# A mixer kernel: channel weights, GpSimd sums and one weight split queued behind named instructions

## The chip, the cores and the metric

The kernel runs on one core of one Trainium2 chip. The metric is device time in microseconds (us), taken as the median of several executions; a profiled execution of the same program gives the span from its first to its last instruction and the trace that is read here.

## The reference, cut to what matters

Eight batches, eight heads, 576 tokens, 64 channels a head. A linear attention (softmax of q over the channels, softmax of k over the tokens) makes x; two small networks follow, one over tokens and one over channels.

```python
q_s = exp(q - max(q, -1)); q_s = q_s / (sum(q_s, -1) + 1e-9)
k_s = exp(k - max(k, 2));  k_s = k_s / (sum(k_s, 2) + 1e-9)
x = q_s @ (k_s^T v)                       # (8, 576, 512) over all heads
h = relu(x^T @ w_tok1) @ w_tok2           # w_tok1 576x256, w_tok2 256x576
u = x + h^T
out = u + relu(u @ w_ch1) @ w_ch2         # w_ch1 512x1536, w_ch2 1536x512
```

The weights arrive as 8-byte numbers, so each piece of them (128x512) has to be narrowed on the chip.

## The kernel before, in words

**Units.** The attention is cut into 32 units, one for a batch and a pair of heads. A unit passes through `softmax_k` and `softmax_q` (VectorE and ScalarE), the transposes and the k-v product (`stage_qT`, `stage_kv`), `stage_y`, `stage_h1`, and two halves of `stage_u`. Each half ends by emptying its PSUM bank into u: a ScalarE copy makes the high part uh (L365), a VectorE subtraction the low part ul (L366). The first eight units are "early": they run in a loop of their own, before any step of the channel network is issued, with buffers of their own (`early_pools`).

**Steps.** The tokens are cut into nine groups of 512. For a group g and a block f of 128 hidden channels, `ch1(g, f)` does 12 matmuls into a bank and drains it into h2h (ScalarE, L379) and h2l (VectorE, L380); `ch2` does 12 more matmuls, one step later. The steps run in the order (0, 0..3), (1, 0..11), (0, 4..11), then groups 2 to 8. At the end of the first four steps the sums of group zero are copied to `part` (L409); the rest of group zero is added at its end. Units 8 to 31 are spread over the steps by a table (`todo`).

**Weights.** `load_ch(f)` loads the pieces of w_ch1 and w_ch2 for block f. For each piece there is a DMA into `stg` issued by SyncE (L154), then `narrow` (VectorE L162, ScalarE L163, VectorE L164, L165, L167, L169), then `split` into a high and a low part (ScalarE L102, VectorE L103). Blocks 0 and 1 are loaded in the early loop, after units 5 and 6; blocks 2 to 11 are loaded at the steps 0 to 9, one at each. Step 4 + f is the first that needs a block f of 4 or more. `split_tok1` splits w_tok1, which the early units use whole, for the later units; it stands after unit 4 in the loop.

**Sums on GpSimd.** `residual` makes u = uh + ul ready for the output. For group one and later it is one GpSimd addition for each quarter into a `stg` buffer (L402). For group zero it is two for each quarter, into `part` (L395, L396).

**Order.** The program's text gives priorities. A scheduler with its own timeline orders each engine's queue: it lets an instruction go ahead of earlier text when its engine would be free and its data ready in that timeline. On the chip each engine then keeps to its queue's order.

Of the kernel before, what the change touches and what calls it, by code (L numbers as in the profile page):

```python
# [1 line left out]

# [6 lines left out]
F32 = mybir.dt.float32  # L9
F32R = mybir.dt.float32r  # L10
U32 = mybir.dt.uint32
AF = mybir.ActivationFunctionType
ALU = mybir.AluOpType
AX = mybir.AxisListType

P = 128
# [4 lines left out]
def attn_mixer_kernel(ctx: ExitStack, tc: tile.TileContext, q, k, kt, v, wt, out, dims):  # L21
# [3 lines left out]
    nc = tc.nc  # L25
    B, H, S, D, TOK, DM, DCH, wide = dims
    NJ = DM // P
    NF = DCH // P
# [7 lines left out]
    NE = 2 * NJ  # L36
    F_HEAD, F_MORE = 4, 8

    const = ctx.enter_context(tc.tile_pool(name="const", bufs=1))
    sm = ctx.enter_context(tc.tile_pool(name="sm", bufs=2))  # L40
    stg = ctx.enter_context(tc.tile_pool(name="stg", bufs=2))
    cv = ctx.enter_context(tc.tile_pool(name="cv", bufs=2))
# [42 lines left out]
    def c2_rows(f0, f1):  # L85
        late = ctx.enter_context(tc.tile_pool(name=f"late{f0}", bufs=1))
        h_ = late.tile([P, f1 - f0, DM], F32R, name=f"c2h{f0}")
        l_ = late.tile([P, f1 - f0, DM], F32R, name=f"c2l{f0}")
        for f in range(f0, f1):
            c2[f] = h_[:, f - f0, :], l_[:, f - f0, :]  # L90
# [6 lines left out]
    def f32(ap):  # L97
        return ap.bitcast(F32)

    def split(hi, lo, src, lo_eng):  # L100

        nc.scalar.copy(hi, src)  # L102
        lo_eng.tensor_tensor(lo, src, f32(hi), op=ALU.subtract)  # L103
# [3 lines left out]
    def ps_unit(dtype=F32):  # L107

        pools = unit_banks[0]
        pool, name = pools[turn[0] % len(pools)]  # L110
        turn[0] += 1
        return pool.tile([P, 512], dtype, name=name)
# [33 lines left out]
    def load_weights(i, n=CW, out=None):  # L146

        if not wide:
            t = out if out is not None else cv.tile([P, C1 * P], F32, name="cv_s")[:, 0:n]
            nc.sync.dma_start(t, wt[i][:, 0:n])  # L150
            return t
        conv.append(conv.pop(0))
        raw = conv[-1][0].tile([P, CW, 2], U32, name="stg")
        nc.sync.dma_start(raw[:, 0:n, :].rearrange("p n w -> p (n w)"), wt[i][:, 0:n].bitcast(U32))  # L154
        return narrow(raw, n, out)
# [30 lines left out]
    def split_tok1():  # L186
        split(w1h, w1l, w1f[:, 0:C, :], nc.vector)
        split(w1th, w1tl, w1t, nc.vector)

    def load_tok2():  # L190
        for n in range(NT):
            split(w2h[:, n, 0:S0], w2l[:, n, 0:S0], load_weights(AT_T2 + n), nc.vector)
        t = load_weights(AT_TAIL + 1, NT * TL).rearrange("p (n t) -> p n t", n=NT)
        split(w2h[:, :, S0:S], w2l[:, :, S0:S], t, nc.vector)

    def load_ch(f):
        h_, l_ = (w[:, f].rearrange("p n m -> p (n m)") for w in (c1h, c1l))
        split(h_, l_, load_weights(AT_C1 + f), nc.vector)
        split(*c2[f], load_weights(AT_C2 + f), nc.vector)
# [137 lines left out]
    uT = [slots[i] for i in (0, 1, 2, 1, 0, 2, 1, 0, 2)]  # L337
    assert len(uT) == NG

    def stage_u(u, half):  # L340
        b, j = u["b"], u["j"]
        edge = (b + 1) * CW - b * S
        cut = min(max(edge, S - 320), 320)
        n0, n1 = ((0, cut), (cut, S))[half]
        N = n1 - n0
        ns = slice(n0, n1)
        t = ps_unit()
        if u["early"]:
            mm = [(u["kvf"], u["qt"][:, ns])]
        else:  # L350
            mm = [(u["kvh"], u["qth"][:, ns]), (u["kvh"], u["qtl"][:, ns]), (u["kvl"], u["qth"][:, ns])]
        for n in range(NT):
            mm += [
                (u["hh"][:, n, :], w2h[:, n, ns]),
                (u["hh"][:, n, :], w2l[:, n, ns]),
                (u["hl"][:, n, :], w2h[:, n, ns]),
            ]
        for i, (a, w) in enumerate(mm):
            nc.tensor.matmul(t[:, 0:N], a, w, start=(i == 0), stop=(i == len(mm) - 1))  # L359
        for g, a0, a1 in ((b, n0, min(n1, edge)), (b + 1, max(n0, edge), n1)):  # L360
            if a0 < a1:
                at = b * S + a0 - g * CW
                uh, ul = (x[:, j, at : at + a1 - a0] for x in uT[g])
                src = t[:, a0 - n0 : a1 - n0]
                nc.scalar.copy(uh, src)  # L365
                nc.vector.tensor_tensor(ul, src, f32(uh), op=ALU.subtract)  # L366


    def ch1(g, f):
        hh = hpool.tile([P, CW], F32R, name="h2h")  # L370
        hl = hpool.tile([P, CW], F32R, name="h2l")
        t = ps_h.tile([P, 512], F32, name="ps_h")
        i = 0
        for n in range(NJ):
            uh, ul = (x[:, n, :] for x in uT[g])
            for a, w in ((c1h, uh), (c1l, uh), (c1h, ul)):
                nc.tensor.matmul(t, a[:, f, n, :], w, start=(i == 0), stop=(i == 3 * NJ - 1))  # L377
                i += 1
        nc.scalar.activation(hh, t, AF.Relu)  # L379
        nc.vector.scalar_tensor_tensor(hl, t, 0.0, f32(hh), op0=ALU.max, op1=ALU.subtract)  # L380
        return hh, hl

    def ch2(acc, f, first, last, hh, hl):

        for n, o in enumerate(acc):
            cs = slice(n * P, (n + 1) * P)
            for i, (a, w) in enumerate(((c2[f][0], hh), (c2[f][1], hh), (c2[f][0], hl))):
                nc.tensor.matmul(o, a[:, cs], w, start=(first and i == 0), stop=(last and i == 2))  # L388

    def residual(g, n):  # L390

        uh, ul = (x[:, n, :] for x in uT[g])
        if g == 0:
            t = part[:, n, :]
            nc.gpsimd.tensor_tensor(t, t, f32(uh), op=ALU.add)  # L395
            nc.gpsimd.tensor_tensor(t, t, f32(ul), op=ALU.add)  # L396
            res[n] = t
            return
        if n % 2 == 0:
            t = stg.tile([P, CW, 2], U32, name="stg").rearrange("p n w -> p (n w)").bitcast(F32)  # L400
            res[n], res[n + 1] = t[:, 0:CW], t[:, CW : 2 * CW]
        nc.gpsimd.tensor_tensor(res[n], f32(uh), f32(ul), op=ALU.add)  # L402

    res = {}

    def out_end(g, acc, whole):
        for n, o in enumerate(acc):
            if not whole:
                nc.scalar.copy(part[:, n, :], o)  # L409
                continue  # L410
            nc.vector.tensor_tensor(res[n], o, res[n], op=ALU.add)
            nc.scalar.dma_start(out[g, n], res[n])
# [4 lines left out]
    def begin(n):  # L417
        if n < NU and n not in units:
            units[n] = load_unit(n // NJ, n % NJ)

    def soft(n):
        if n < NU:
            softmax_k(units[n])
            softmax_q(units[n])

    def pe_stages(n):
        def s1():
            stage_qT(units[n])
            stage_kv(units[n])

        def s2():
            stage_y(units[n])

        def s3():
            stage_h1(units[n])
            stage_u(units[n], 0)

        def s4():
            stage_u(units[n], 1)

        return s1, s2, s3, s4
# [19 lines left out]
    for n in range(NE):  # L461
        st = pe_stages(n)
        st[0]()
        st[1]()
        if n == 0:
            load_tok2()
        if n + 2 < NE:
            begin(n + 2)
            soft(n + 2)
        st[2]()  # L470
        st[3]()
        if n == NE - 4:
            split_tok1()
        if NE - 3 <= n < NE - 1:
            load_ch(n - (NE - 3))
    early_pools.close()
    del v_ring[1:], kv_ring[1:]
    ld = ctx.enter_context(tc.tile_pool(name="ld", bufs=2))
# [35 lines left out]
            put(x, fn)  # L514

    pend = None
    to_load = 2
    for i, (g, f) in enumerate(steps):
        if to_load < NF and (i < F_HEAD or g == 1):
            if to_load == F_MORE:  # L520
                more_pools.close()
                conv[:] = [(stg, cv)]
                c2_rows(F_MORE, NF)
            load_ch(to_load)
            to_load += 1
        h = ch1(g, f)
        for fn in todo.pop(i, []):
            fn()
        if pend is not None:
            ch2(*pend[1:])  # L530
            if pend[0] != g:
                out_end(*pend[:2], i != F_HEAD)
        for fn in todo.pop(i + 0.5, []):
            fn()
        last = i + 1 == len(steps) or steps[i + 1][0] != g
        if pend is None or pend[0] != g:
            acc = [ps_o.tile([P, CW], F32, name="ps_o") for _ in range(NJ)]
        pend = (g, acc, f, pend is None or pend[0] != g, last, *h)
        if last and i != F_HEAD - 1:
            for n in range(NJ):  # L540
                residual(g, n)
# [60 lines left out]
```

## Time and profile before

| what | value |
|---|---|
| median of 3 runs | 851.43 us (850.38 to 853.24) |
| profiled execution, its own time | 851.01 us |
| span of its instructions | 849.2 us |
| mean granted TensorE clock | 0.995 |
| busy: TensorE, VectorE, ScalarE, GpSimd | 807.7, 495.6, 323.8, 132.5 us |
| chain that ended last: TensorE, VectorE, DMA | 76%, 14%, 5% |

The engines are called PE (TensorE matmuls), PEld (its weight loads), DVE (VectorE), ACT (ScalarE), POOL (GpSimd) and SP (SyncE). A row of the timeline gives the start, the time taken, engine, line, operation, output<-input and the count of merged instructions; in brackets stand the idle time of the engine before it and what ended it. A DVE instruction's time is some 0.07 us longer than the distance to the next one's start when it runs undisturbed, since neighbours overlap.

### The profile page before, as it was taken

What the parts mean: (1) busy time and instruction counts of PE and PEld (TensorE: products, weight loads), DVE (VectorE), ACT (ScalarE), POOL (GpSimd) and SP (SyncE); (2) the same over time, 40 slices, a digit from 0 to 9 for tenths busy, and PEclk for the clock granted to TensorE, in tenths of its full rate; (3) what the DMA queues carried; (4) which work ended last, traced back from release to release, by engine and by line L of the source; (5) the groups of instructions that cost most, each with busy time, mean ns of one, the idle gap of its engine ahead of it and who ended that gap; (6) DMA issues with size and microseconds to landing.
All of it is one profiled execution on the core that took longest, in us unless ns stands there. A gap on an engine that the chain in (4) does not pass through costs nothing.

```text
span 849.2 us, 11727 instructions
## 1 busy us (share of the span) xinstructions
PE 807.7 (95%) x4464; PEld 671.8 (79%) x4464; DVE 495.6 (58%) x1076; ACT 323.8 (38%) x749; POOL 132.5 (16%) x104
## 2 busy tenths in 40 slices
PE   3779997998999999999999999999999999999997
PEld 2567885877888888888888888888888888888885
DVE  7899899988665555565557555755566322112111
ACT  4576552444553444344434344444344321011110
POOL 0000015042221111131113011311131102001000
PEclk9999999999999999999999999999999999999999
DMA  8543742223223222322213122312131001001001
GB/s 264 171 137 93 237 136 81 93 76 110 62 77 95 61 61 61 110 61 61 61 40 97 51 60 61 98 58 61 46 95 46 15 1 50 1 0 50 1 1 50
DMA packets 60632, 63.54 MB, mean 75 GB/s; under 512 B 40864, under 2 KB 40992, under 8 KB 60576
## 3 DMA queue, kind: packets, MB, share of 16 engines
q1 hardware_dynamic: 55392, 53.36, 21.5%
q10 hardware_dynamic: 5184, 9.44, 3.0%
q8 instruction: 35, 0.57, 0.3%
q14 instruction: 21, 0.17, 0.1%
HBM read 53.35 MB, written 9.44 MB: 74 GB/s over the span
## 4 chain that ended last, share of the span: by engine, by line
PE 76%; DVE 14%; DMA 5%; issue 2%; ACT 1%; POOL 1%; DVEq 0%; SPq 0%; POOLq 0%
PE ps_h L377 29%; PE ps_o L388 29%; PE ps_h L359 7%; PE ps_h L316 5%; PE ps_h L256 2%; DMA stg<-in_w 2%; DMA q_t<-in_q 2%; DVE q_t L302 2%; DVE stg L167 2%; DVE cv_s L169 1%; PE ps_h L324 1%; DVE cv_s L164 1%; DMA out<-stg 1%; PE ps_h L222 1%; DVE stg L165 1%
## 5 line engine op out<-in xcount | busy, mean ns | idle before, releaser
L380 DVE SCALAR_TENSOR_TENSOR h2l<-ps_h,h2h 128x512 fp32r<-128x512 f32 x108 | 74.0, 686 | 177.0 <-ACT h2h L379 177.0
L388 PE MATMUL ps_o<-h2h,c2h 128*128 128x512 f32 x432 | 169.9, 396 | 4.4 <-ACT h2h L379 4.4
L377 PE MATMUL ps_h<-uh,c1h 128*128 128x512 f32 x432 | 171.3, 396 | 0.0
L377 PE MATMUL ps_h<-ul,c1h 128*128 128x512 f32 x432 | 170.9, 396 | 0.0
L377 PE MATMUL ps_h<-uh,c1l 128*128 128x512 f32 x432 | 170.4, 394 | 0.0
L388 PE MATMUL ps_o<-h2h,c2l 128*128 128x512 f32 x432 | 169.8, 393 | 0.0
L379 ACT ACTIVATE h2h<-ps_h 128x512 fp32r<-128x512 f32 x108 | 64.3, 596 | 248.3 <-PE ps_h L377 240.7
L388 PE MATMUL ps_o<-h2l,c2h 128*128 128x512 f32 x432 | 154.6, 396 | 2.3 <-DVE h2l L380 2.3
L302 DVE COPY q_t<-cv_s 32x160 f32<-32x160 f32 (+1 forms) x264 | 72.8, 276 | 63.5 <-POOL ql L103 60.2
L388 PEld LDWEIGHTS ps_o<-h2h,c2h 128*128 128x128 f32 x432 | 81.7, 189 | 22.2 <-ACT h2h L379 5.3
L377 PEld LDWEIGHTS ps_h<-ul,c1h 128*128 128x128 f32 x432 | 81.3, 188 | 19.3
L388 PEld LDWEIGHTS ps_o<-h2l,c2h 128*128 128x128 f32 x432 | 79.6, 188 | 19.9 <-DVE h2l L380 3.6
L388 PEld LDWEIGHTS ps_o<-h2h,c2l 128*128 128x128 f32 x432 | 81.7, 189 | 16.8
L377 PEld LDWEIGHTS ps_h<-uh,c1h 128*128 128x128 f32 x432 | 81.3, 188 | 17.1
L377 PEld LDWEIGHTS ps_h<-uh,c1l 128*128 128x128 f32 x432 | 81.5, 189 | 16.8
L225 POOL TENSOR_TENSOR k_t<-k_t,mb 128x640 f32<-128x640 f32 x24 | 37.8, 1574 | 280.4 <-ACT mb L224 280.3
L402 POOL TENSOR_TENSOR stg<-uh,ul 128x512 f32<-128x512 f32 x32 | 41.6, 1324 | 155.8 <-DMA out<-stg 76.8
L103 POOL TENSOR_TENSOR ql<-q_t,qh 128x640 fp32r<-128x640 f32 x24 | 37.9, 1580 | 96.6 <-ACT qh L102 59.7
L233 DVE TENSOR_REDUCE st<-q_t 128x10 f32<-128x640 f32 x32 | 26.2, 818 | 42.5 <-DMA q_t<-in_q 42.5
L235 ACT ACTIVATE q_t<-q_t 128x640 f32<-128x640 f32 x32 | 23.6, 739 | 49.0 <-DVE q_t L234 49.0
L302 ACT COPY q_t<-cv_s 32x128 f32<-32x128 f32 (+1 forms) x120 | 36.8, 307 | 1.5
L359 PE MATMUL ps_h<-w2h,hh 128*128 128x256 f32 (+1 forms) x112 | 33.1, 303 | 1.4 <-ACT hh L331 1.4
(140 smaller groups left out, 1162.1 us busy)
## 6 DMA issues: line engine op xcount, KB each, us to landing
stg<-in_w SPq DMA_DIRECT2D x28, 512.0 KB, 3.7
kt_t<-in_kt SPq DMA_DIRECT2D x32, 320.0 KB, 3.5
q_t<-in_q SPq DMA_DIRECT2D x32, 320.0 KB, 3.0
v_t<-in_v SPq DMA_DIRECT2D x64, 128.0 KB, 3.0
out<-stg ACTq DMA_DIRECT2D x32, 256.0 KB, 2.7
k_t<-in_k SPq DMA_DIRECT2D x24, 320.0 KB, 3.6
v_t<-in_v SPq DMA_DIRECT2D x32, 32.0 KB, 3.1
out<-part ACTq DMA_DIRECT2D x4, 256.0 KB, 4.6
```

Source lines behind the costliest of these rows:

```text
L103: lo_eng.tensor_tensor(lo, src, f32(hi), op=ALU.subtract)
L225: nc.gpsimd.tensor_tensor(kx, kx, mb.unsqueeze(1).broadcast_to([P, C1, P]), op=ALU.subtract)
L233: nc.vector.tensor_reduce(st[:, 0, :], qt, axis=AX.X, op=ALU.max)
L235: nc.scalar.activation(qc, qc, AF.Exp)
L302: eng(qx[ys, 0:n, xs], turned[xs, 0:n, ys])
L316: nc.tensor.matmul(y[:, 0:TOK], a, w, start=(i == 0), stop=(i == len(mm) - 1))
L359: nc.tensor.matmul(t[:, 0:N], a, w, start=(i == 0), stop=(i == len(mm) - 1))
L377: nc.tensor.matmul(t, a[:, f, n, :], w, start=(i == 0), stop=(i == 3 * NJ - 1))
L379: nc.scalar.activation(hh, t, AF.Relu)
L380: nc.vector.scalar_tensor_tensor(hl, t, 0.0, f32(hh), op0=ALU.max, op1=ALU.subtract)
L388: nc.tensor.matmul(o, a[:, cs], w, start=(first and i == 0), stop=(last and i == 2))
L402: nc.gpsimd.tensor_tensor(res[n], f32(uh), f32(ul), op=ALU.add)
```

## The change

Four places change. A tiny exponential on a scratch tile is issued first of all. The scheduler is then told, with `issue_after`, that certain instructions follow a named one on the same engine's queue: `split_tok1` and the loads of blocks 0 and 1 stand behind the last emptying of the unit before them; each later load stands behind the draining of the step before it; the sums of group zero stand behind the last sum of group one. `issue_after` binds an instruction only to the named instruction of its own engine, so the loads' DMAs, issued by SyncE, are not bound. Last, blocks 6 to 11 are loaded at steps 4, 6, 7, 9, 10 and 12 instead of 4 to 9.

```diff
+    warm = const.tile([P, 1], F32, name="warm")
+    nc.gpsimd.memset(warm, 0.0)
+    nc.scalar.activation(warm, warm, AF.Exp)
...
+    emptied = []
...
-                nc.scalar.copy(uh, src)
-                nc.vector.tensor_tensor(ul, src, f32(uh), op=ALU.subtract)
+                emptied[:] = [
+                    nc.scalar.copy(uh, src).ins,
+                    nc.vector.tensor_tensor(ul, src, f32(uh), op=ALU.subtract).ins,
+                ]
+    drained = []
+    @contextmanager
+    def behind(instructions):
+        with ExitStack() as stack:
+            for ins in instructions:
+                stack.enter_context(tc.issue_after(ins))
+            yield
...
-        nc.scalar.activation(hh, t, AF.Relu)
-        nc.vector.scalar_tensor_tensor(hl, t, 0.0, f32(hh), op0=ALU.max, op1=ALU.subtract)
+        drained[:] = [
+            nc.scalar.activation(hh, t, AF.Relu).ins,
+            nc.vector.scalar_tensor_tensor(hl, t, 0.0, f32(hh), op0=ALU.max, op1=ALU.subtract).ins,
+        ]
...
-            nc.gpsimd.tensor_tensor(t, t, f32(uh), op=ALU.add)
-            nc.gpsimd.tensor_tensor(t, t, f32(ul), op=ALU.add)
+            with behind(joined):
+                nc.gpsimd.tensor_tensor(t, t, f32(uh), op=ALU.add)
+                nc.gpsimd.tensor_tensor(t, t, f32(ul), op=ALU.add)
...
-        nc.gpsimd.tensor_tensor(res[n], f32(uh), f32(ul), op=ALU.add)
-    res = {}
+        joined[:] = [nc.gpsimd.tensor_tensor(res[n], f32(uh), f32(ul), op=ALU.add).ins]
+    res, joined = {}, []
...
-        if n == NE - 4:
-            split_tok1()
-        if NE - 3 <= n < NE - 1:
-            load_ch(n - (NE - 3))
+        with behind(emptied):
+            if n == NE - 4:
+                split_tok1()
+            if NE - 3 <= n < NE - 1:
+                load_ch(n - (NE - 3))
...
-    to_load = 2
+    load_at = dict(zip((0, 1, 2, 3, 4, 6, 7, 9, 10, 12), range(2, NF)))
     for i, (g, f) in enumerate(steps):
-        if to_load < NF and (i < F_HEAD or g == 1):
-            if to_load == F_MORE:
+        if i in load_at:
+            if load_at[i] == F_MORE:
                 more_pools.close()
                 conv[:] = [(stg, cv)]
                 c2_rows(F_MORE, NF)
-            load_ch(to_load)
-            to_load += 1
+            with behind(drained):
+                load_ch(load_at[i])
```

More of the change, by code (lines that the diff above doesn't have):

```diff
@@ L1 @@
-from contextlib import ExitStack
+from contextlib import ExitStack, contextmanager
 import concourse.bass as bass
```

## The prediction

> **What bounds the kernel now.** I read the page first, for its busy shares and the slices of the span.
>
> ```profile
> span 849.2 us, 11727 instructions
> PE   3779997998999999999999999999999999999997
> DVE  7899899988665555565557555755566322112111
> PE 76%; DVE 14%; DMA 5%; issue 2%; ACT 1%; POOL 1%; DVEq 0%; SPq 0%; POOLq 0%
> ```
>
> From the tenth slice on PE is busy nearly always, and no order of the other engines can shorten what it has to do. The first ten slices, some 210 us, are where DVE is full and PE is not. So I cut that stretch with the windows view (columns: window, its length, busy time and count of PE, PEld, DVE, ACT and POOL, granted clock, DMA share, GB/s).
>
> ```profile
> 45.00:66.00 21.00, 15.61 (x121) 13.09 (x120) 19.54 (x49) 14.88 (x38) 0.00 (x0) 1.00 0.43 125
> 66.00:89.00 23.00, 22.28 (x177) 19.31 (x178) 21.07 (x50) 15.08 (x40) 0.00 (x0) 1.00 0.32 96
> 89.00:131.00 42.00, 42.00 (x189) 34.53 (x188) 40.53 (x73) 18.91 (x35) 7.43 (x5) 1.00 0.53 175
> 131.00:144.00 13.00, 7.75 (x27) 5.67 (x26) 13.00 (x15) 3.78 (x7) 7.70 (x5) 0.87 0.28 97
> 144.00:187.00 43.00, 43.00 (x211) 34.90 (x210) 41.20 (x72) 18.64 (x36) 9.29 (x6) 1.00 0.26 80
> 187.00:200.00 13.00, 8.89 (x43) 6.68 (x42) 9.93 (x25) 5.06 (x14) 1.57 (x1) 1.00 0.26 98
> 200.00:350.00 150.00, 150.00 (x892) 127.50 (x890) 90.36 (x216) 66.21 (x160) 27.25 (x18) 1.00 0.25 72
> ```
>
> After 200 us PE has no idle time. Before, it idles 5.4 us in 45 to 66 (21.00 less 15.61), 5.25 us in 131 to 144 (13.00 less 7.75), and 4.1 us in 187 to 200. Everything that this change can win or lose is PE time in these stretches, or in the two full ones between them. Two timelines tell who holds PE in the second stretch.
>
> ```profile
> 133.14 1.19 PE L388 MATMUL ps_o<-h2l,c2h 128*128 128x512 f32 x4 [1.42 <-DVE h2l L380]
> 140.94 0.80 PE L388 MATMUL ps_o<-h2h,c2h 128*128 128x512 f32 x1 [3.83 <-ACT h2h L379]
> 143.24 0.63 PE L388 MATMUL ps_o<-h2h,c2l 128*128 128x512 f32 x1
> 134.24 0.62 ACT L102 CAST c2h<-cv_s 128x512 fp32r<-128x512 f32 x1 [7.73 <-POOL part L395]
> 139.68 0.72 ACT L163 ACTIVATE cv_s<-cv_s,ebias 128x512 uint32<-128x512 uint32 x1 [4.49 <-DVE cv_s L162]
> 123.57 5.23 POOL L395 TENSOR_TENSOR part<-part,uh 128x512 f32<-128x512 f32 x3 [120.72 <-ACT part L409]
> 133.57 5.13 POOL L396 TENSOR_TENSOR part<-part,ul 128x512 f32<-128x512 f32 x3
> 124.03 1.78 DVE L164 SCALAR_TENSOR_TENSOR cv_s<-stg,cv_s 128x512 uint32<-128x512 uint32 x1
> 129.27 3.21 DVE L165 TENSOR_SCALAR stg<-stg 128x512 uint32<-128x512 uint32 x2
> 132.41 0.68 DVE L380 SCALAR_TENSOR_TENSOR h2l<-ps_h,h2h 128x512 fp32r<-128x512 f32 x1
> 139.17 0.41 DVE L162 TENSOR_SCALAR cv_s<-stg 128x512 uint32<-128x512 uint32 x1
> ```
>
> PE waits for the draining (h2h), ACT's queue has a conversion ahead of it that waits for DVE, and DVE runs at a third of its speed: L164 takes 1.78 us and two L165 take 3.21, exactly while GpSimd makes group zero's sums (123.57 to 138.7). Only the draining L380, which reads PSUM, keeps its 0.68. Ten DVE instructions start between 124.03 and 139.17, 15.1 us; these are the undisturbed distances of the same kinds:
>
> ```profile
> 152.94 0.68 DVE L164 SCALAR_TENSOR_TENSOR cv_s<-stg,cv_s 128x512 uint32<-128x512 uint32 x1
> 153.54 0.68 DVE L103 TENSOR_TENSOR c2l<-cv_s,c2h 128x512 fp32r<-128x512 f32 x1
> 154.15 0.41 DVE L165 TENSOR_SCALAR stg<-stg 128x512 uint32<-128x512 uint32 x1
> ```
>
> From one start to the next is 0.60 for the long ones, 0.34 for a 0.41. The ten would need some 5.6 us (seven of 0.60, two of 0.34, one softmax product of 0.73). So the sums cost DVE 9.5 us, and through ACT's queue they cost PE its 5.25 us of idle time, plus a slow restart: the clock is 0.87 in that window, and eight matmuls from 140.94 on come some 0.43 us apart where 0.23 is usual, 1.8 us more. That is 7 us of PE.
>
> **The change part by part.** Sums are made against the profiled execution, 851.0 us with 849.2 of span; the median of the runs, 851.4, lies 0.4 above it.
>
> *The scratch exponential: 0.* It pulls one table load forward:
>
> ```profile
> 3.96 1.28 ACT L209 ACT_TABLE_LOAD   x1 [3.96 <-DMA kt_t<-in_kt]
> 5.26 0.83 ACT L209 ACTIVATE kt_t<-kt_t,mc 128x640 f32<-128x640 f32 x1
> 4.77 0.15 DVE L208 TENSOR_SCALAR mc<-mc 128x1 f32<-128x1 f32 x1
> ```
>
> The first exponential could start at 4.95 instead of 5.26, 0.3 us, less than the 0.4 between the profiled run and the median. I take nothing; the bounds are -0.3 and 0.
>
> *The split of w_tok1: -0.7.* The scheduler had pulled it forward to the first microseconds:
>
> ```profile
> 20.23 1.21 DVE L103 TENSOR_TENSOR w1l<-w1f,w1h 128x1024 fp32r<-128x1024 f32 x1
> 29.38 0.40 DVE L103 TENSOR_TENSOR w1tl<-w1t,w1th 128x256 fp32r<-128x256 f32 x1
> 77.83 0.28 DVE L366 TENSOR_TENSOR ul<-ps_o,uh 128x128 fp32r<-128x128 f32 x1
> ```
>
> It now follows unit 4's last subtraction, the row at 77.83. Of the 1.6 us of DVE that leave the start, the second part is on the chain of waits, just ahead of a q transfer; the first is followed by a wait for a k transfer, which eats most of it. I take -0.7, between 0 and -1.6. At its new place, in 66 to 89, PE is the full engine and nothing waits for the result before unit 8; it costs nothing there. Were it in the way, it would cost its 1.6 again.
>
> *Blocks 0 and 1 out of the early units: -4.* Their conversions run from the 43rd microsecond, in between the softmaxes of units 2 to 5:
>
> ```profile
> 55.28 0.68 DVE L169 TENSOR_TENSOR cv_s<-stg,cv_s 128x512 f32<-128x512 f32 x1
> 57.19 0.38 PE L324 MATMUL ps_h<-kvf,ys 128*128 128x128 f32 x1 [1.65 <-ACT kvf L266]
> 84.68 0.28 DVE L366 TENSOR_TENSOR ul<-ps_h,uh 128x128 fp32r<-128x128 f32 x1
> 91.57 0.28 DVE L366 TENSOR_TENSOR ul<-ps_o,uh 128x128 fp32r<-128x128 f32 x1
> 89.13 0.58 PE L377 MATMUL ps_h<-uh,c1h 128*128 128x512 f32 x1
> ```
>
> One sees it at 55.28: DVE and then ACT convert a channel weight, behind it comes kvf, and PE starts 1.65 us late. A piece is six DVE instructions, four of 0.60 and two of 0.34, so 3.1 us, and a block 6.2. After the change they follow the subtractions at 84.68 (unit 5) and 91.57 (unit 6). PE's idle time in 45 to 66 is 5.4 us, the most that can come back; a part of it is the units' own latency, so I take -4, between 0 and -5.4. With this and the split, unit 5 is emptied near 80.0 instead of 84.68, and PE could start the first step near 84.4 instead of 89.13.
>
> *The same work paid later: +3.5.* From 80.0 on, DVE has blocks 0 to 3 to convert, eight pieces, beside the ends of units 6 and 7. The first piece needs its whole latency (six DVE and two ACT instructions in turn, about 5 us), so PE waits some 0.6 us at the first step. A step takes PE
>
> ```profile
> 740.62 2.80 PE ps_h L377 x12
> 743.42 2.76 PE ps_o L388 x12
> ```
>
> 5.56 us, while DVE needs 6.2 for a block and 0.6 for the draining, 6.8. Three more steps that need a fresh block make 3 x 1.2 = 3.6, less what units 6 and 7 still give PE to do. I take +3.5 in all; the low bound is 0, the high one 12.4 (the difference at all ten loaded steps). From step 4 on a block is loaded three or more steps ahead, and at steps 5, 8 and 11 nothing is loaded: 5.56 us for DVE to catch up each time. SyncE's queue is not bound and still fetches as `stg` buffers come free; a piece late there delays the q and k transfers of units 8 and 9 behind it, which have until step 12.
>
> *The sums of group zero out of the loading steps: -6.5.* They go behind group one's last sum, to 175 us or later. PE gets back at most the 7 us worked out above; I keep half a microsecond for the conversions that still crowd DVE there. The bounds are 0 and -7.
>
> *The sums at their new place: +2.* Eight additions fall into 175 to 205, where unit 8's copies already meet group one's sums:
>
> ```profile
> 178.33 5.08 DVE L302 COPY q_t<-cv_s 32x160 f32<-32x160 f32 x11
> 212.03 2.73 DVE L302 COPY q_t<-cv_s 32x160 f32<-32x160 f32 x11 [0.58 <-POOL ql L103]
> ```
>
> 5.08 us against 2.73 a unit later, 2.4 us for three meetings or so. But DVE has 3.1 us free in 187 to 200 and 40% of its time from 200 on (90.36 of 150.00), and PE after 200 did not notice. I take +2, between 0 and +9.5 (the price at the old place), nearer to zero because the result is not needed for eight steps.
>
> The Trainium skill speaks against this part: "SBUF — State Buffer", section "Who interferes with whom", has the shared port pair of DVE and GpSimd as an exclusive lock, held for a whole instruction, which DVE instructions with two SBUF inputs and two-port copies need too. By that rule moving the sums removes none of the blocking, it only chooses other victims, and the sum would be +9.5 here instead of +2. The rows at 124.03 and 132.41 agree with the lock and with the exemption of a single SBUF input; what it costs PE is another question, since it depends on who waits.
>
> Sum: 0 - 0.7 - 4 + 3.5 - 6.5 + 2 = -5.7, so 845.3 against the profiled 851.0, and with the 0.4 between profile and median about 845.5.
>
> **The rivals.**
>
> *A, the loads march in step with PE: slower, 854.* Bound behind the draining of the step before, a load can no longer run ahead, and DVE's 6.8 us for a loaded step replaces PE's 5.56 at all ten, 12.4 us in place of 3.5: 845.3 + 8.9 = 854.2. For it: DVE is busy 40.53 of 42.00 and 41.20 of 43.00 us, with no reserve. Against it: 9.5 of those microseconds are the sums' blocking, and the lead of three steps. It decides from the point where step i's draining stands behind the last conversion of load i in DVE's or ACT's queue.
>
> *B, the blocking only moves: no change, 852.8.* The sums hold up unit 8's and 9's copies and GpSimd's own ql and k work, PE's 4.1 us of idle time in 187 to 200 grow: 845.3 - 2 + 9.5 = 852.8. For it: the copies at 178.33. Against it: DVE's free time there. That the order doesn't change at all is excluded: w1l stood at 20.23, and may not now.
>
> *C, nothing is paid later: 840.* Units 6 and 7 give PE 12 us of work during which DVE has little else, so blocks 0 and 1 hide wholly (845.3 - 3.5 = 841.8), and the sums cost nothing (839.8). For it: DVE's own work for these two units is small. Against it: blocks 2 and 3 follow at once.
>
> **How the numbers follow.** My forecast (842.5 to 849) has 0.46, C 0.22, B 0.14, A 0.18. The bound for telling a change from none is 0.3%, 2.55 us. Faster takes the forecast and C, 0.68; the same takes B and a little of A, 0.15; slower the rest of A, 0.17. The range reaches to C with some of the stall of 187 to 200 gone, 836, and to A, 854; the likeliest case's own is 842 to 849.
>
> **What would show it.** Right: no DVE instruction of 1.7 us or more between 90 and 165, and no PE gap over 3 us there; w1l after 70 us; the first L377 near 85; part's additions behind the fourth L402 of group one. Wrong: the first L377 still at 89, gaps ahead of L377 or L388 in the first four steps that sum to more than 4 us, gaps between 175 and 205 of more than 7 us, or drainings that wait in every loaded step.

## The result: 1% slower, and the profile after

The changed kernel takes 859.84 us (median of 6 runs, 857.53 to 864.4) against 850.9 of the kernel before on the same chip: a ratio of 1.0105, 95% interval 1.0072 to 1.0138. The forecast was 845.5, with a range from 836 to 854. Ratios compare fast runs alone, so one of the twelve runs of e6 below, at 1152.69 us, is left out of its ratio (its median would be 850.14 without it). The profiled execution took 857.53 us, with a span of 855.7, 6.5 more than before. Lines of the code have moved by three to nineteen: the conversions are L165 to L172 and L105/L106 now, the steps L393 and L406, the sums of group zero L414/L415.

First the page: the span, the slices of PE and VectorE, and the chain's shares.

```profile
span 855.7 us, 11725 instructions
PE   3898689997999999999999999999999999999997
DVE  7976999898865555575547555655557322112112
PE 80%; DVE 12%; DMA 4%; ACT 1%; issue 1%; SPq 0%; POOL 0%; DVEq 0%; ACTq 0%; POOLq 0%
```

PE's 7 at 127 to 149 us has become a 9, but the fifth slice, 86 to 107 us, shows a 6 and the next an 8 where there were 9s. VectorE's two 9s in the third and fourth slice (43 to 86 us) are a 7 and a 6. The windows of the prediction, asked of the changed kernel (same columns):

```profile
45.00:66.00 21.00, 20.32 (x151) 17.13 (x149) 15.04 (x42) 12.68 (x37) 0.00 (x0) 1.00 0.28 78
66.00:89.00 23.00, 20.81 (x140) 17.99 (x141) 15.19 (x37) 13.10 (x34) 0.00 (x0) 0.93 0.19 48
89.00:131.00 42.00, 30.13 (x115) 22.85 (x114) 40.35 (x76) 17.91 (x31) 2.11 (x1) 0.84 0.52 176
131.00:144.00 13.00, 13.00 (x58) 10.63 (x57) 12.54 (x25) 7.70 (x14) 0.00 (x0) 1.00 0.38 121
144.00:187.00 43.00, 43.00 (x205) 34.91 (x205) 38.09 (x67) 17.43 (x33) 6.36 (x4) 1.00 0.34 108
187.00:200.00 13.00, 11.45 (x57) 8.97 (x57) 12.02 (x17) 4.97 (x10) 11.23 (x8) 1.00 0.18 50
200.00:350.00 150.00, 146.22 (x859) 124.06 (x858) 96.57 (x229) 66.64 (x163) 32.06 (x22) 0.99 0.26 75
```

PE gained in 45 to 66 (20.32 busy for 15.61) and in 131 to 144 (13.00 for 7.75), and lost in 89 to 131: 11.87 us idle where it had none. The timeline of PE says in front of what, and who ended each wait:

```profile
68.19 0.71 PE L327 MATMUL ps_h<-kvf,ys 128*128 128x128 f32 x4 [2.68 <-ACT kvf L269]
...
84.69 0.58 PE L393 MATMUL ps_h<-uh,c1h 128*128 128x512 f32 x1
...
93.86 0.50 PE L393 MATMUL ps_h<-uh,c1l 128*128 128x512 f32 x1 [1.43 <-DVE c1l L106]
97.38 0.50 PE L406 MATMUL ps_o<-h2h,c2h 128*128 128x512 f32 x1 [0.69 <-ACT h2h L396]
100.45 1.21 PE L406 MATMUL ps_o<-h2l,c2h 128*128 128x512 f32 x4 [0.96 <-DVE h2l L397]
108.78 0.79 PE L393 MATMUL ps_h<-uh,c1h 128*128 128x512 f32 x1 [7.12 <-ACT c1h L105]
111.24 1.22 PE L393 MATMUL ps_h<-uh,c1h 128*128 128x512 f32 x2 [1.67 <-ACT c1h L105]
```

The first step starts at 84.69 (89.13 before). Then the steps of blocks 1, 2 and 3 wait for their weights, 1.43 + 0.69 + 0.96 + 7.12 + 1.67 = 11.87 us; with the slow restarts after the gaps (granted clock 0.84 in that window) it is some 16 us against the matmuls' usual distances (0.23 us from one 128x512 matmul to the next). So the books, reckoned in that way, after less before, are: first step -4.4, this stretch +16.2, 131 to 144 -7.3, 187 to 210 +2.8, together +7.3; the spans differ by 6.5.

Why c1h came so late stands in VectorE's queue (its timeline: a wait, and then softmax instructions of units 8 and 9, L236 and L237, among the pieces of blocks 2 and 3):

```profile
74.27 0.49 DVE L372 TENSOR_TENSOR ul<-ps_o,uh 128x320 fp32r<-128x320 f32 x1 [4.43 <-ACT uh L371]
...
93.92 0.81 DVE L236 TENSOR_REDUCE st<-q_t 128x10 f32<-128x640 f32 x1
94.65 0.68 DVE L106 TENSOR_TENSOR c2l<-cv_s,c2h 128x512 fp32r<-128x512 f32 x1
95.25 0.42 DVE L165 TENSOR_SCALAR cv_s<-stg 128x512 uint32<-128x512 uint32 x1
96.57 0.82 DVE L236 TENSOR_REDUCE st<-q_t 128x10 f32<-128x640 f32 x1 [0.90 <-DMA q_t<-in_q]
97.30 0.82 DVE L237 TENSOR_TENSOR q_t<-q_t,st 128x640 f32<-128x640 f32 x1
...
107.40 0.67 DVE L172 TENSOR_TENSOR cv_s<-stg,cv_s 128x512 f32<-128x512 f32 x1
```

A piece starts at 95.25, and the first product of any of the four is there at 107.40, because softmaxes and pieces take turns. But that is the near cause. The far one is in what VectorE had done by then. In the kernel before, the last instruction of a piece (c1l or c2l) shows eight pieces done by 96.65: blocks 0 and 1 whole, and the c1 halves of blocks 2, 3, 4 and 5 (by the order of loading; a row names no block). From 80 us on, before and after:

```profile
82.46 0.69 DVE L103 TENSOR_TENSOR c1l<-cv_s,c1h 128x512 fp32r<-128x512 f32 x1
84.95 0.68 DVE L103 TENSOR_TENSOR c1l<-cv_s,c1h 128x512 fp32r<-128x512 f32 x1
90.63 0.68 DVE L103 TENSOR_TENSOR c1l<-cv_s,c1h 128x512 fp32r<-128x512 f32 x1
95.96 0.69 DVE L103 TENSOR_TENSOR c1l<-cv_s,c1h 128x512 fp32r<-128x512 f32 x1
```
```profile
81.77 0.69 DVE L106 TENSOR_TENSOR c1l<-cv_s,c1h 128x512 fp32r<-128x512 f32 x1
83.05 0.69 DVE L106 TENSOR_TENSOR c2l<-cv_s,c2h 128x512 fp32r<-128x512 f32 x1 [0.59 <-ACT c2h L105]
93.12 0.68 DVE L106 TENSOR_TENSOR c1l<-cv_s,c1h 128x512 fp32r<-128x512 f32 x1
94.65 0.68 DVE L106 TENSOR_TENSOR c2l<-cv_s,c2h 128x512 fp32r<-128x512 f32 x1
113.15 0.68 DVE L106 TENSOR_TENSOR c1l<-cv_s,c1h 128x512 fp32r<-128x512 f32 x1
```

After, four pieces are done by 95.33: VectorE is four pieces, 12.4 us, behind. The same lag is there by 85.7, as the first steps begin: six pieces against two. Most of it is idle time and not other work. In 45 to 89 VectorE was busy 19.54 + 21.07 = 40.61 of 44 us before. The windows of the changed kernel for 45 to 89, and from the start to unit 8's `hl` (VectorE's half of the draining ahead of unit 8's stage_u, L335, which matters below):

```profile
45.00:89.00 44.00, 41.13 (x291) 35.12 (x290) 30.24 (x78) 25.77 (x69) 0.00 (x0) 0.96 0.23 62
0.00:204.93 204.93, 167.30 (x928) 135.22 (x928) 176.69 (x352) 101.62 (x216) 26.79 (x33) 0.96 0.43 136
```

13.76 us idle (44.00 less 30.24) in place of 3.39, so 10.4 more. One of these waits, the 4.43 us ahead of 74.27, is the binding at work: the next conversion had to follow unit 5's emptying, and VectorE stood still until that came.

### The profile page after: what moved, and what is told of

Same layout as the page of the kernel before. It is cut to its first block, busy times and chain, and to the rows that moved or that the text cites. A ratio compares the mean times of both kernels' runs of the same rounds, so it can differ in the third digit from the quotient of the medians.

```text
span 855.7 us, 11725 instructions
## 1 busy us (share of the span) xinstructions
PE 811.5 (95%) x4464; PEld 673.5 (79%) x4464; DVE 495.0 (58%) x1076; ACT 325.1 (38%) x750; POOL 131.0 (15%) x105
## 4 chain that ended last, share of the span: by engine, by line
PE 80%; DVE 12%; DMA 4%; ACT 1%; issue 1%; SPq 0%; POOL 0%; DVEq 0%; ACTq 0%; POOLq 0%
PE ps_h L393 31%; PE ps_o L406 29%; PE ps_h L364 7%; PE ps_h L319 5%; PE ps_h L259 2%; DMA stg<-in_w 2%; DMA q_t<-in_q 2%; PE ps_h L327 1%; DVE cv_s L167 1%; DVE q_t L305 1%; PE ps_o L364 1%; PE ps_o L319 1%; DVE stg L170 1%; PE ps_h L225 1%; DVE cv_s L172 1%
## 5 line engine op out<-in xcount | busy, mean ns | idle before, releaser
L393 PE MATMUL ps_h<-uh,c1h 128*128 128x512 f32 x432 | 173.0, 401 | 8.8 <-ACT c1h L105 8.8
L393 PE MATMUL ps_h<-uh,c1l 128*128 128x512 f32 x432 | 171.3, 397 | 1.4 <-DVE c1l L106 1.4
L393 PE MATMUL ps_h<-ul,c1h 128*128 128x512 f32 x432 | 171.7, 398 | 0.0
L406 PE MATMUL ps_o<-h2h,c2h 128*128 128x512 f32 x432 | 170.4, 395 | 0.9 <-ACT h2h L396 0.9
L406 PE MATMUL ps_o<-h2h,c2l 128*128 128x512 f32 x432 | 169.4, 392 | 1.3 <-DVE c2l L106 1.3
L406 PE MATMUL ps_o<-h2l,c2h 128*128 128x512 f32 x432 | 154.0, 396 | 1.2 <-DVE h2l L397 1.2
L393 PEld LDWEIGHTS ps_h<-uh,c1h 128*128 128x128 f32 x432 | 82.1, 190 | 26.9 <-ACT c1h L105 9.7
L393 PEld LDWEIGHTS ps_h<-ul,c1h 128*128 128x128 f32 x432 | 81.9, 190 | 19.5
L393 PEld LDWEIGHTS ps_h<-uh,c1l 128*128 128x128 f32 x432 | 82.2, 190 | 19.0 <-DVE c1l L106 1.9
L406 PEld LDWEIGHTS ps_o<-h2h,c2h 128*128 128x128 f32 x432 | 81.4, 188 | 18.9 <-ACT h2h L396 2.0
L406 PEld LDWEIGHTS ps_o<-h2h,c2l 128*128 128x128 f32 x432 | 81.3, 188 | 18.3 <-DVE c2l L106 1.6
L406 PEld LDWEIGHTS ps_o<-h2l,c2h 128*128 128x128 f32 x432 | 79.5, 188 | 18.2 <-DVE h2l L397 2.0
L106 POOL TENSOR_TENSOR ql<-q_t,qh 128x640 fp32r<-128x640 f32 x24 | 38.1, 1588 | 194.5 <-ACT qh L105 159.5
L236 DVE TENSOR_REDUCE st<-q_t 128x10 f32<-128x640 f32 x32 | 26.2, 818 | 40.0 <-DMA q_t<-in_q 39.9
L238 ACT ACTIVATE q_t<-q_t 128x640 f32<-128x640 f32 x32 | 23.7, 740 | 52.2 <-DVE q_t L237 49.8
```

The costliest lines, as they stand in the source:

```text
L236: nc.vector.tensor_reduce(st[:, 0, :], qt, axis=AX.X, op=ALU.max)
L238: nc.scalar.activation(qc, qc, AF.Exp)
```

## The experiments

All were timed in rounds against the kernel before, run on the same chip. The kernel before took 852.01 us in the rounds of e1 to e4, 852.02 in those of e5 to e8, 852.75 for e9 to e12 and 852.07 for e13 to e15; the table's 850.9 belongs to the rounds of the changed kernel. So kernels of different rounds are compared below by their ratios: 0.001 is 0.85 us, and a difference of two ratios is uncertain by some 2.5 us. The last three columns are of the profiled executions: when unit 8's `hl` started, how long VectorE had been idle until then (that time less its busy time in the window from 0), and what was left of the span.

| kernel | median us | ratio to before (95%) | unit 8's `hl` | VectorE idle ahead | span less `hl` |
|---|---|---|---|---|---|
| before | 850.9 | | 199.23 | 17.9 | 650.0 |
| changed | 859.84 | 1.0105 (1.0072 to 1.0138) | 204.93 | 28.2 | 650.8 |
| e1_early_free | 854.03 | 1.0021 (0.9996 to 1.0046) | 198.02 | 25.1 | 652.2 |
| e2_soft_late | 859.48 | 1.0106 (1.0041 to 1.0171) | 202.57 | 26.1 | 652.5 |
| e3_sums_only | 854.27 | 1.0023 (1.0004 to 1.0042) | 200.04 | 19.3 | 653.2 |
| e4_no_sums | 861.59 | 1.0105 (1.006 to 1.015) | 207.14 | 26.1 | 651.1 |
| e5_sums_vector | 844.36 | 0.9915 (0.9893 to 0.9937) | 191.19 | 19.4 | 652.0 |
| e6_free_vector | 850.19 | 0.9979 (0.9965 to 0.9993) | 195.86 | 26.1 | 650.7 |
| e7_after_vector | 855.35 | 1.0029 (1.0011 to 1.0048) | 201.37 | 28.1 | 652.4 |
| e8_early_bound | 863.67 | 1.0136 (1.0114 to 1.0159) | 214.12 | 31.6 | 650.9 |
| e9_split_only | 844.23 | 0.9907 (0.9887 to 0.9927) | 191.76 | 18.5 | 650.2 |
| e10_drained_only | 846.52 | 0.9938 (0.9917 to 0.996) | 194.85 | 25.4 | 647.9 |
| e11_loads01_bound | 857.64 | 1.0055 (1.0036 to 1.0074) | 202.75 | 28.2 | 650.2 |
| e12_soft9_late | 847.75 | 0.9938 (0.9915 to 0.9961) | 182.97 | 23.7 | 662.3 |
| e13_bound_soft_late | 852.78 | 1.0003 (0.9978 to 1.0027) | 195.68 | 26.2 | 652.7 |
| e14_load1_bound | 863.2 | 1.0128 (1.0099 to 1.0156) | 209.88 | 33.4 | 650.5 |
| e15_vector_old_place | 849.75 | 0.9966 (0.995 to 0.9982) | 196.69 | 19.1 | 651.2 |

The last column is nearly constant, but for e12. By itself that is bookkeeping: PE is full behind unit 8, and in most of these kernels the same 928 matmuls stand ahead of it. In the same way the start of `hl` is VectorE's busy time plus its idle time, whatever the cause. The columns say where to look, at what brings unit 8's `hl` earlier or later; only an edit can show what does.

**Four first cuts: one part undone, one part alone.**

e1_early_free, the change without the binding of blocks 0 and 1:

```diff
-            if NE - 3 <= n < NE - 1:
-                load_ch(n - (NE - 3))
+        if NE - 3 <= n < NE - 1:
+            load_ch(n - (NE - 3))
```

> The changed kernel with the loads of blocks 0 and 1 not bound behind units 5 and 6; all else of the change stays. Theory 'lost DVE time' (binding these loads leaves DVE idle in 45 to 84 us and starts the conversions too late): PE's loss of some 16 us in 84 to 120 goes almost wholly, the first L393 is back near 89 instead of 84.7 (4.4 us lost), so 859.8 - 16 + 4.4 = 848. Rival 'softmaxes first' (DVE's queue has the softmaxes of units 8 and 9, 8.7 us, ahead of blocks 2 and 3): these stay, about half of the stall stays, 855.

e2_soft_late, the change with unit 8's softmax bound behind the fifth step's draining and unit 9's behind the ninth's:

```diff
-        soft(NE)
+        with behind(drains[4]):
+            soft(NE)
...
-        put(at[0], lambda n=n: soft(n + 1))
+        def s0(n=n):
+            with behind(drains[8] if n == NE else []):
+                soft(n + 1)
+        put(at[0], s0)
```

> The changed kernel with the softmax of unit 8 bound behind the draining of step 4 and that of unit 9 behind step 8; the loads stay bound as changed. 'Softmaxes first': PE's loss in 84 to 120 falls from 16 us by about the 8.7 us of softmax and a little of the slow clock, 859.8 - 9 = 851. 'Lost DVE time': blocks 2 and 3 are late anyway, the loss falls by 2 to 3 us, 857.

e3_sums_only, the kernel before with nothing but the sums' binding:

```diff
+            with behind(joined):
                 nc.gpsimd.tensor_tensor(t, t, f32(uh), op=ALU.add)
                 nc.gpsimd.tensor_tensor(t, t, f32(ul), op=ALU.add)
```

> The kernel before with one part of the change alone: the sums of group zero behind the last sum of group one. If the two traces are read rightly, PE's 7.2 us in 131 to 144 come back and 187 to 210 gets 2 to 3 us worse: 851 - 4.5 = 846.5. If the blocking only moves: 851.

e4_no_sums, the change without it:

```diff
-            with behind(joined):
+            with behind([]):
```

> The changed kernel without the order of the sums. If the sums are worth 4.5 us in any company: 859.8 + 4.5 = 864. If the starving of the first steps leaves DVE slack where the sums would fall: 860, no difference.

In e1 and e2 the stall of 89 to 120 is gone or small (PE loses some 1 and 4.5 us there in place of 16), as it should be if blocks 0 and 1 and the softmaxes cause it, and in e3 the one of 131 to 144 is gone; and yet none of the three gets under the kernel before. e1 and e3 missed their theories of 848 and 846.5 by 6 and 8 us, and e2 lies above both of its values. In all three another stall has opened at unit 8. Its place in e3, in VectorE's, GpSimd's and PE's timeline:

```profile
169.91 12.93 DVE L302 COPY q_t<-cv_s 32x160 f32<-32x160 f32 x11
197.30 2.71 DVE L302 COPY q_t<-cv_s 32x160 f32<-32x160 f32 x11
...
168.17 2.98 POOL L410 TENSOR_TENSOR stg<-uh,ul 128x512 f32<-128x512 f32 x2 [1.23 <-DVE cv_s L169]
171.10 5.03 POOL L403 TENSOR_TENSOR part<-part,uh 128x512 f32<-128x512 f32 x4
176.09 1.56 POOL L225 TENSOR_TENSOR k_t<-k_t,mb 128x640 f32<-128x640 f32 x1
177.60 4.92 POOL L404 TENSOR_TENSOR part<-part,ul 128x512 f32<-128x512 f32 x4
...
184.35 0.79 PE L395 MATMUL ps_o<-h2l,c2h 128*128 128x512 f32 x1 [6.95 <-DVE h2l L387]
```

Unit 8's eleven copies, 2.71 us when GpSimd is idle, take 12.93: GpSimd is busy without a break from 169.91 to 182.5, and about one copy gets through per GpSimd instruction (12.93 / 11 = 1.18 us, an addition there takes 1.25). Behind the copies the draining waits, and PE 6.95 us. e1 has the same (11 copies in 9.58 us) and e2 (12.51 us). e4 shows the other side: with the sums back at 129 to 144 their stall is back (2.53 us of PE idle at 145.16), and the time is no better.

**The sums off GpSimd.** e5_sums_vector, the kernel before with the eight additions on VectorE, behind unit 11's emptying (`emptied` is kept as in the change):

```diff
-            nc.gpsimd.tensor_tensor(t, t, f32(uh), op=ALU.add)
-            nc.gpsimd.tensor_tensor(t, t, f32(ul), op=ALU.add)
+            with behind(emptied):
+                nc.vector.tensor_tensor(t, t, f32(uh), op=ALU.add)
+                nc.vector.tensor_tensor(t, t, f32(ul), op=ALU.add)
```

> The kernel before, with group zero's eight additions on VectorE instead of GpSimd, bound behind unit 11's emptying (some 230 us). Theory (a GpSimd addition holds every short VectorE copy that meets it, and unit 8's eleven copies are the costly place): the 7.25 us that PE loses in 131 to 144 go, nothing comes back at 175 to 200, where the loss stays near 5, and eight additions of some 0.6 us lie where VectorE has time: about 844. Rival (VectorE's queue up to unit 8 is what binds, and any stall taken out comes back at unit 8): a gap of about 7 us ahead of a step between 175 and 200, and 851 to 854, as when the additions stayed on GpSimd behind group one's sums (854.3).

e6_free_vector and e7_after_vector have the same edit on e1 and on the changed kernel.

> The changed kernel with the loads of blocks 0 and 1 unbound and group zero's eight additions on VectorE behind unit 11's emptying. Theory of the copies: without the additions on GpSimd (854.0) the gap of 7.59 at 189.70 shrinks to 2 or 3, so some 5 us less: 848 to 849, below the kernel before. Rival (VectorE's queue binds as a whole): 853 to 854, the gap stays.

> The changed kernel, with only group zero's eight additions moved to VectorE behind unit 11's emptying. The stall of 16 us in 89 to 120 should be as in the changed kernel, since the additions were never there, and 187 to 210 should lose 5 instead of 7.9: about 856.5. Against the kernel before with the same additions on VectorE the difference is the price of the loads' order alone: 11 to 12 us if the reading of the windows holds; under 5 if the stall in 89 to 120 merely uses time that unit 8 would have lost anyway.

844.36 us: e5 beats both kernels, and nothing came back at unit 8. It changes the engine and the place of the additions at once. On VectorE near their old place they win 0.34% (e15 below, 0.9966) of e5's 0.85%; no run has them on GpSimd behind unit 11. Its `hl` is 8 us earlier, and VectorE's additions lie at 246 us, beside nothing that waits (timeline and window of VectorE's columns from 0 to `hl`):

```profile
170.09 5.07 DVE L302 COPY q_t<-cv_s 32x160 f32<-32x160 f32 x11
...
246.03 3.06 DVE L407 TENSOR_TENSOR part<-part,uh 128x512 f32<-128x512 f32 x4
```
```profile
0.00:191.19 191.19, 161.80 (x928) 133.22 (x928) 171.77 (x363) 100.48 (x215) 16.03 (x24) 0.99 0.45 146
```

e7, of the same rounds, is 11.0 us slower than e5 (855.35 against 844.36; 9.7 by the ratios): the price of the loads' order, the scratch exponential included, with the sums out of the way on both sides. e6 came out at 850.19, a little above its theory.

**The loads' order in its parts.** e8_early_bound is the kernel before with only the binding behind the emptying (split and blocks 0 and 1), sums at their old place:

```diff
-        if n == NE - 4:
-            split_tok1()
-        if NE - 3 <= n < NE - 1:
-            load_ch(n - (NE - 3))
+        with behind(emptied):
+            if n == NE - 4:
+                split_tok1()
+            if NE - 3 <= n < NE - 1:
+                load_ch(n - (NE - 3))
```

> The kernel before, with only the split of w_tok1 and the loads of blocks 0 and 1 bound behind the emptying; the other loads and the additions as before. Theory (with blocks 0 and 1 late, the softmaxes of units 8 and 9 stand ahead of blocks 2 and 3 on VectorE, and PE waits): the first step at 84.5, 10 us or more lost in 89 to 120, the 7 us of 131 to 144 partly hidden in it: 855 to 860. Rival (it is the binding of the later loads behind the draining that keeps blocks 2 and 3 late): less than 4 us lost in 89 to 120, and 847 to 849.

863.67 us, above its theory's 855 to 860. The gap of the changed kernel is there to a hundredth, without any binding behind a draining, and the sums' stall comes 10 us later (PE's timeline):

```profile
109.72 0.80 PE L388 MATMUL ps_h<-uh,c1h 128*128 128x512 f32 x1 [7.13 <-ACT c1h L102]
...
150.48 0.80 PE L399 MATMUL ps_o<-h2h,c2h 128*128 128x512 f32 x1 [4.43 <-ACT h2h L390]
```

e9, e10 and e11 split the order up on e5: the split alone behind `emptied`; blocks 2 to 11 alone at the changed steps, behind `drained`; blocks 0 and 1 alone behind `emptied`.

```diff
 e9
+        with behind(emptied if n == NE - 4 else []):
             if n == NE - 4:
                 split_tok1()
 e10
-        if to_load < NF and (i < F_HEAD or g == 1):
+        if i in load_at:
...
-            load_ch(to_load)
-            to_load += 1
+            with behind(drained):
+                load_ch(load_at[i])
 e11
+        with behind(emptied):
             if NE - 3 <= n < NE - 1:
                 load_ch(n - (NE - 3))
```

> The kernel before with the additions on VectorE (844.4), and of the order of the loads only the binding of w_tok1's split behind unit 4's emptying. If the split is worth what the prediction took, 0.7 us less: 843.7. Rival: at its new place its two casts on ScalarE stand ahead of unit 5's kvf, PE waits 2.7 us there as at 68.19 of the changed kernel, and it is 846 to 847.

> The kernel before with the additions on VectorE (844.4), and only blocks 2 to 11 loaded at the changed kernel's steps, each behind the draining of the step before. If the split is the cheap part and this binding holds conversions back, 848 to 850: with the blocks 0 and 1 unbound, the changed order costs 850.2 - 844.4 = 5.8 us, and all but the split's share of it would be here. Rival: the binding is free, because a load still runs three steps ahead, 844 to 845, and the split has the 5.8.

> The kernel before with the additions on VectorE (844.4), and only blocks 0 and 1 bound behind the emptying of units 5 and 6. Theory (these two blocks are what was dear: their twelve microseconds of VectorE work leave a stretch where VectorE then idles, and come back ahead of the first steps): a gap of 5 us or more ahead of a step between 95 and 115, unit 8's hl some 8 us later than 191.2, and 852 to 854. Rival (the stall needs the later loads bound too, or the split): under 848.

Against e5's 0.9915: the split 0.9907, 0.7 us less; the draining 0.9938, 2.0 us more (the intervals of both overlap with e5's); blocks 0 and 1 1.0055, 11.9 us more (13.3 by the medians). With 857.64 us e11 lies above its theory of 852 to 854. Its timeline of PE has the same gap (its profiled execution, 854.73 us, is its fastest, so the table's `hl` shows less than the medians do):

```profile
107.33 0.79 PE L388 MATMUL ps_h<-uh,c1h 128*128 128x512 f32 x1 [7.14 <-ACT c1h L102]
```

So the binding of two blocks' loads is the change's loss. e6 (split, draining and scratch exponential together) is 5.5 above e5 where the first two alone give 1.3; the remainder is not far above the uncertainty, and it is not explained here.

**Idle time or softmaxes?** e13_bound_soft_late is e11 with the softmaxes of units 8 and 9 bound as in e2. e14_load1_bound is e5 with block 1 alone bound. e15_vector_old_place is e5 with the additions told to follow group one's sums. Those run on GpSimd, and `issue_after` binds an instruction only to a named one of its own engine, so on VectorE nothing holds the additions: they start at 126.83, ahead of group one's first sum at 170.23, and land amid the conversions, near the place that GpSimd's additions had.

```diff
 e14
+        with behind(emptied if n == NE - 2 else []):
             if NE - 3 <= n < NE - 1:
                 load_ch(n - (NE - 3))
 e15
-            with behind(emptied):
+            with behind(joined):
                 nc.vector.tensor_tensor(t, t, f32(uh), op=ALU.add)
```

> Blocks 0 and 1 bound behind the emptying, additions on VectorE (857.6 so), and in addition the softmaxes of units 8 and 9 bound behind the drainings of the fifth and the ninth step. If those softmaxes are the cause, the gap of 7.14 at 107.33 goes for good and the time falls to 844 to 847. Rival (VectorE's idle time in 45 to 89, some 11 us in place of 4, is lost for good): the gap goes, another of the same size opens between 160 and 205, unit 8's hl stays near 202, and it is 853 to 857.

> Additions on VectorE (844.4), and only block 1 bound behind unit 6's emptying; block 0 stays where the scheduler puts it. If the lost idle time of VectorE is the price, half the moved work costs about half: 849 to 851. Rival (a threshold: the price comes only when the first step itself waits for its block): 844 to 846.

> The eight additions on VectorE as in the kernel of 844.4, but ordered behind group one's sums as in the changed kernel; in VectorE's queue they then stand amid the conversions, at some 125 us, instead of behind unit 11. That is 4.8 us of VectorE work more ahead of unit 8, and nothing else. If VectorE's queue up to unit 8 sets the time, it shows one for one: 849. Rival (the idle time of VectorE behind 144 absorbs it): 844 to 846.

VectorE from 45 to 89 in e5, e11, e13 and e14, a window row each:

```profile
45.00:89.00 44.00, 38.02 (x299) 32.53 (x299) 39.82 (x99) 29.00 (x74) 0.00 (x0) 1.00 0.34 103
```
```profile
45.00:89.00 44.00, 41.92 (x319) 36.13 (x318) 32.98 (x83) 25.78 (x67) 0.00 (x0) 1.00 0.23 63
```
```profile
45.00:89.00 44.00, 42.32 (x321) 36.43 (x320) 32.38 (x82) 26.43 (x70) 0.00 (x0) 1.00 0.25 67
```
```profile
45.00:89.00 44.00, 40.24 (x308) 34.54 (x309) 28.45 (x75) 25.26 (x69) 0.00 (x0) 1.00 0.25 69
```

Idle: 4.2, 11.0, 11.6 and 15.6 us. e13 keeps 7.5 of e11's 11.9 us and so comes nearest to its rival, though `hl` is at 195.68 and not near 202: with the softmaxes out of the way the third step no longer waits 7 us, and unit 8 waits instead (3.00 for qth at 191.13, 2.12 for h2h at 176.14). The softmaxes in front are worth some 4.4 us, and the rest stays without them. e14 went against its expectation: half the moved work cost more, 18.1 us. It also idles more, because block 0 alone is converted early (c1l at 57.21, c2l at 61.20) and then VectorE has no conversion at all until 87.46; by 97.1 four pieces are done, as in e11. In these runs the price follows not how much is bound but how long VectorE is left with nothing it may do.

e15 turns the sign: VectorE work added, nothing idle. The timeline shows the additions, and the window from 0 to `hl`:

```profile
126.83 1.89 DVE L403 TENSOR_TENSOR part<-part,uh 128x512 f32<-128x512 f32 x3
...
135.16 0.68 DVE L404 TENSOR_TENSOR part<-part,ul 128x512 f32<-128x512 f32 x1
```
```profile
0.00:196.69 196.69, 164.88 (x928) 135.50 (x928) 177.62 (x367) 100.08 (x215) 17.48 (x24) 0.97 0.45 141
```

VectorE's busy time ahead of `hl` is 5.9 us more than in e5, its idle time the same; `hl` is 5.5 later and the time 4.3 by the ratios (5.4 by the medians). So work added to VectorE's queue up to unit 8 is paid nearly one for one, and idle time there goes with a loss at least as large in two kernels: 8.8 us more of it in e11 with 11.9 us, 14.0 in e14 with 18.1. It is not a law: e10 idles 6.0 more than e5 and loses only 2.0, with eight matmuls more done ahead of `hl`; by 85.7 us it is only one piece behind e5, five against six.

e12_soft9_late tried to use that: unit 9's softmax behind unit 8's `hl`, on e5 (`split_of` keeps the instruction of `hl`).

```diff
-        put(at[0], lambda n=n: soft(n + 1))
+        if n == NE:
+            late = at[2]
+        else:
+            put(at[0], lambda n=n: soft(n + 1))
...
+        if n == NE:
+            def soft9(n=n):
+                with behind(split_of[n]):
+                    soft(n + 1)
+            put(late, soft9)
```

> The kernel before with the additions on VectorE (844.4), and unit 9's softmax bound behind unit 8's hl, instead of standing amid the conversions at 104 to 125. In nine kernels so far the span ended 650 to 653 us after unit 8's hl, so what stands ahead of that instruction on VectorE would set the time: seven instructions, some 4 us, go behind it, and the time is 840 to 841. Rival (VectorE waits there anyhow, and unit 9 comes late and holds up PE): 844 to 850, with a new gap between 195 and 215.

It missed its theory. Unit 8 was 8 us earlier (`hl` at 182.97), and units 9 and 10 became the late ones, unit 9 in the place that the rival had named (PE's timeline, a wait of each):

```profile
204.55 0.63 PE L364 MATMUL ps_h<-qth,kvh 128*128 128x320 f32 x1 [2.98 <-ACT qth L102]
...
229.87 0.42 PE L364 MATMUL ps_h<-w2h,hl 128*128 128x320 f32 x1 [1.45 <-DVE hl L334]
```

So unit 8's `hl` sets the time only as long as unit 8 is the late one.

## Why the prediction was wrong

**The step that failed is "the same work paid later: +3.5".** In the changed kernel's 89 to 120 it measured 16.2 us, above even the high bound of 12.4. e11, which has the gain at the first step in it as well, is 11.9 us slower than e5, where the terms of -4 and +3.5 promised 0.5 less. The forecast set VectorE's 6.8 us for a loaded step against PE's 5.56 and charged the difference per step. That takes for granted that VectorE stands where it stood at the first step. It did not: of the eight pieces that the forecast lists as still to convert from 80 us on, the kernel before has six done by 85.7 us and the changed one two, and most of the missing 12.4 us was VectorE's idle time in 45 to 89 (10.4 us more). The trace of before showed it: c1l for blocks 2 and 3 at 82.46 and 84.95, before the first step. Two blocks were bound, and the pieces of four came late. In e11 no load but those two is bound, and yet the third c1l, block 2's, comes at 111.70 (e5: 82.31). I take the weights' buffers for the reason, which go round in the order of the program. The changed kernel's trace agrees: SyncE fetches no weight between 41.40 and 81.11 us, and the fetch at 81.11 follows the last reading of block 0's first piece (L172, 80.41 to 81.09). No run gave the weights more buffers. The softmaxes of units 8 and 9, given "until step 12", were a second miss of the same step: the scheduler had them at 92 to 112, amid and ahead of the pieces of blocks 2 and 3 (worth some 4.4 us by e13).

**Blocks 0 and 1 out of the early units, -4:** right. PE's first step came at 84.69, forecast 84.4.

**The split, -0.7:** right in size, though not clear of the uncertainty (e9: 0.7 us under e5 by the ratios). That it "costs nothing there" was not right in detail: its casts stand on ScalarE ahead of unit 5's kvf, and PE waits 2.68 us at 68.19; in e9 the same wait of 2.66 did not show in the time. It stood at 67.33, a little ahead of the 70 us that I had named.

**The sums out of the loading steps, -6.5:** right. 131 to 144 is full, a gain of 7.3, and no VectorE instruction takes 1.7 us between 90 and 165 but one of 2.02 at 110.47, which meets GpSimd's ql. The working's 1.8 us for the slow restart is 1.5 by the starts at 140.94 and 144.06, seven distances of 0.23 and 3.12 us in all; the sum does not hang on it.

**The sums at their new place, +2:** +2.8 in the changed kernel, but for a reason that I had not: unit 8 was late there and met the sums' end. In e3 the price was about that of rival B: its terms, -6.5 and +9.5, make 3 us more than before, and e3 took 2.0 more by its ratio. The blocking only moved. The rule cited from the Trainium skill ("SBUF — State Buffer", "Who interferes with whom") was the better guide: e3's copies agree with it, held by each GpSimd instruction in turn, at 12.93 us for 2.71. I chose +2 because of 3.1 us of free VectorE time in 187 to 200, and did not ask which instructions would meet the sums.

**The scratch exponential, 0:** not run alone.

Of the rivals, A with 854.2 came nearest to the changed kernel's 859.84, but not by its mechanism: the loads bound behind the draining cost about 2.0 us (e10), where A had 8.9 more than the forecast. Of the signs of being right, the first step near 85 and the place of the additions came, and a gap of 7.12 us stood where none was to pass 3. Of the signs named as wrong, the gaps ahead of the first four steps came, 11.87 us; those of 175 to 205 did not pass 7.

## What to carry to other kernels

Where an in-order engine is the one that sets the end of a stretch, ask of a delayed load not what it releases but what that engine will do in its place; if the answer is nothing, the idle time can come back later, here with more than its length in e11 and e14 and with a third of its length in e10, and whatever is queued behind the load comes later too. Count the lead at the start of the stretch (pieces done, before and after), not only the rate within it. And moving work that blocks another engine is worth what its new victims cost: moving the additions to VectorE and behind unit 11 took 0.85% off the time (e5), moving them on GpSimd to 171 us took nothing off (e3).

## What the hardware showed that I had not expected

In these traces the price of meeting GpSimd went by how many VectorE instructions met it, and hardly by their length. Eleven copies of a quarter microsecond each, 2.71 to 2.73 us alone, took 12.93 us in e3, 0.93 more a copy, and 9.58 in e1 and 12.51 in e2. At the sums' old place ten instructions, most of them of 0.6 us, lost 9.5 us, about as much each. For its amount of work, a row of short copies was the dearest thing to put there.
